# Attention and experts: all eight units in the attention loop, the first expert prepared inside it, POOL's small DMAs issued one by one

## The chip, the core and the metric

One core of a Trainium2 chip. TensorE (PE) multiplies, VectorE (DVE), ScalarE (ACT) and GpSimd (POOL) do the rest of the arithmetic, SyncE (SP) issues most of the DMAs, POOL the indirect ones. The metric is the device time of one execution in microseconds (us).

## What is computed

```python
def sm_attn(qq, kk, vv):
    s = scale * np.matmul(qq, kk.transpose(0, 1, 3, 2))
    s = s - np.max(s, axis=-1, keepdims=True)
    a = np.exp(s)
    a = a / (np.sum(a, axis=-1, keepdims=True) + 1e-09)
    return np.matmul(a, vv)
p_packed = sm_attn(p, k, v)              # 32 packed rows per head
x = sm_attn(q, p_packed, p_packed)       # 8 batches, 8 heads, 576 rows, 64 wide
# x as (4608, 512): row n is a token
logits = x @ w_gate + modality_bias[modality_id]
e_idx = np.argmax(logits, axis=1)        # 8 experts, one for each token
gate_w = softmax(logits)[arange(N), e_idx]
for e in range(E):
    h = np.maximum(x[e_idx == e] @ w1[e], 0.0)        # 512 to 1024
    out[e_idx == e] = gate_w[e_idx == e, None] * (h @ w2[e])
```

All is float32. With the inputs drawn here experts 4, 5 and 7 receive 2311, 1406 and 891 of the 4608 tokens, the other five none. By pairs of batches: 569 and 583 for experts 4 and 5 in the first pair; 589, 258 and 305 for 4, 5 and 7 in the second; 587 and 565 for 4 and 5 in the third; 566 and 586 for 4 and 7 in the fourth.

## The kernel before, in words

**Attention.** A batch is a *unit*; there are eight. Its steps are generators that emit a few instructions at each `next`: loads of k, q and v (`dk`, `dq`, `dv`, 1152 KB each), transposes of k and q on PE with copies by ACT (`k0..2`, `q0..2`), scores of the packed rows with max and exp (`c0`, `c1`), transposes of the weights (`a0..2`), the product with v (`p0`), its transpose (`t0`), the gate's product (`g0`), scores of q with a softmax of eight DVE steps and one ACT exp (`s0`, `s1`), the product that gives x, three tokens a step (`x0..2`, lines 318 to 333: PE, an ACT copy into the tile `xs`, a DVE copy of the logits into `lt`), and the store of x to the DRAM tensor `x_scr` (`w0`).

**The loop.** `ORDER` (line 353) is an order written out by hand for PE, DVE, ACT and SP: one round of it is one period, `>` is the unit after, `<` the unit before, and `e` is a place where one step of something else is emitted (the dictionary `more`). The loop runs it over six units (`NU = 2 * NA[1]`, line 692) and over the first steps of the two that follow. On the engines named in `manual_schedule` the instructions emitted inside keep their order; instructions emitted later are placed by the planner, also between these.

**Routing.** For each pair of batches `routing` (lines 368 to 428) computes the expert of each token and its place in the list of its expert: DVE steps, two or three small PE products for the ranks, DVE steps, an exp on ACT, and then nine indirect DMAs on POOL (line 420) that write 16 bytes for each of 128 tokens into the DRAM tensor `lst`. All nine are emitted at once.

**Slots.** The expert stage works in slots of 256 rows of one expert. `table_phase` (line 527) makes, with some fifty small DVE operations, a table of the slots that are full by then: table a from the first two pairs of batches (two slots), b from three pairs (four more), c from all (the rest; only here are slots that are not full, and one whose second half alone is filled is a half slot). `first_expert` (line 485) takes the expert with most tokens of the first pair; table a starts there, and the tables that follow start where the one before ended, in ascending order of experts, round. A slot is: `fetch` (line 614: POOL reads 256 rows of the list into `mt` and gathers the tokens into `xt` with four indirect DMAs), `st_x` (transposes into `x_hl` as a sum of two parts), `st_1` (96 products of 128x256; `st_1_half` 64 for a half slot), `st_2` (twice 24 products of 128x512, once for a half slot), and after each 24 an ACT step into `ot` (one buffer) and an indirect DMA of POOL into the output. `sw` loads and splits the weights of the next expert when it changes; `split_w` splits into two parts with ACT and DVE, for the very first W1 with ACT and POOL (line 612).

**The order around the change.** Behind the loop the kernel emits table a, the load of W2, the fetches of slots 0 and 1 and the split of W2, then what is left of units 6 and 7 (a second, shorter order, lines 826 to 831), their routing and the tables b and c, and the slots; the planner interleaves them. Till the end of the second attention part the slots have half the PSUM (`W["nh"] = 2`, one tile each of `ps_t` and `ps_o`). W1 of the first expert is loaded and split in the loop (`split_first`, line 719) as `e` steps.

## Time and profile before

| what | value |
|---|---|
| median of the runs | 676.68 us (676.12 to 677.13) |
| the profiled execution, its own time | 669.55 us |
| its span in the profile | 667.8 us |
| PE busy, share of the span | 590.3 us, 88% |
| PE's weight loads | 508.8 us, 76% |
| DVE, ACT, POOL busy | 254.4, 218.7, 203.0 us |

The span in 40 equal slices of 16.7 us, from the page (a digit is the busy share in tenths, 9 is 90% or more; PEclk is PE's granted clock in tenths of full speed):

```profile
PE   4979868767489978999999999999999999999990
POOL 3010050157652172222321334332233133223340
PEclk9989988967669998999999999999999999999996
DMA  9798896508932911111596212920111111113132
```

The first nine slices are the attention loop over six units. In slices nine to twelve PE's share and its clock are lower and POOL is busy; from slice sixteen on PE is busy throughout, and the transfers are few. Line numbers (L646 and so on) are those of the kernel printed above.

### The profile page before, as it was taken

How to read it: one execution, taken by the hardware profiler on the slowest of the kernel's cores; microseconds unless marked ns; L12 is line 12 of the kernel's file. 1: busy time of each engine (PE TensorE's matmuls, PEld its weight loads, DVE VectorE, ACT ScalarE, POOL GpSimd, SP SyncE). 2: the span in 40 equal slices, each digit the busy share in tenths (PEclk: the TensorE clock that was granted, in tenths of full speed). 3: DMA queues.
4: the chain of work that ended last, by engine and by line, in shares of the span. 5: the costliest groups of instructions: out<-in, count | busy, mean ns of one | idle time of the engine just before them, and what ended most of it. 6: DMA issues, size and time to landing. Idle time of an engine off the chain costs nothing. (4 is left out here: it accounts for less than half of the span.)

```text
span 667.8 us, 13143 instructions
## 1 busy us (share of the span) xinstructions
PE 590.3 (88%) x5108; PEld 508.8 (76%) x5108; DVE 254.4 (38%) x629; ACT 218.7 (33%) x369; POOL 203.0 (30%) x228
## 2 busy tenths in 40 slices
PE   4979868767489978999999999999999999999990
PEld 3657636526368968889888988899899889989980
DVE  2669948949635331112612017311121112012370
ACT  3747745636112202112612127221221222122450
POOL 3010050157652172222321334332233133223340
PEclk9989988967669998999999999999999999999996
DMA  9798896508932911111596212920111111113132
GB/s 297 241 378 322 300 312 194 184 11 251 255 96 75 294 48 60 49 48 33 132 278 207 64 57 87 257 65 34 49 50 48 49 49 42 41 48 49 47 54 34
DMA packets 38334, 86.66 MB, mean 130 GB/s; under 512 B 10400, under 2 KB 10400, under 8 KB 37216
## 3 DMA queue, kind: packets, MB, share of 16 engines
q1 hardware_dynamic: 27920, 63.39, 30.2%
q0 software_dynamic: 9264, 21.94, 11.8%
q8 instruction: 51, 0.84, 0.5%
q14 instruction: 43, 0.35, 0.2%
q10 hardware_dynamic: 1056, 0.15, 0.1%
HBM read 66.22 MB, written 19.24 MB: 128 GB/s over the span
## 5 line engine op out<-in xcount | busy, mean ns | idle before, releaser
L646 PE MATMUL ps_h<-x_hl,w1h 128*128 128x256 f32 x1088 | 203.7, 288 | 5.3 <-issue 4.4
L646 PEld LDWEIGHTS ps_h<-x_hl,w1h 128*128 128x128 f32 x1088 | 174.7, 195 | 11.2 <-issue 8.4
L646 PE MATMUL ps_h<-x_hl,w1l 128*128 128x256 f32 x544 | 156.1, 287 | 4.0 <-issue 4.0
L651 DVE SCALAR_TENSOR_TENSOR hl<-ps_h,hh 128x512 fp32r<-128x512 f32 x68 | 47.0, 691 | 263.9 <-ACT hh L650 258.8
L619 POOL DMA_INDIRECT xt<-x_scr,mt x92 | 91.0, 989 | 106.9 <-DMA mt<-lst 39.1
L680 PE MATMUL ps_o<-w2h,hh 128*128 128x512 f32 x296 | 118.0, 399 | 3.1 <-ACT ot L684 1.9
L680 PE MATMUL ps_o<-w2h,hl 128*128 128x512 f32 x296 | 116.5, 394 | 0.0
L680 PE MATMUL ps_o<-w2l,hh 128*128 128x512 f32 x296 | 115.8, 391 | 0.0
L646 PEld LDWEIGHTS ps_h<-x_hl,w1l 128*128 128x128 f32 x544 | 106.3, 195 | 2.7 <-issue 2.5
L650 ACT ACTIVATE hh<-ps_h 128x512 fp32r<-128x512 f32 x68 | 40.6, 597 | 172.1 <-PE ps_h L646 153.7
L685 POOL DMA_INDIRECT out_dram<-ot,mt x37 | 40.8, 1103 | 149.4 <-ACT ot L684 90.1
L684 ACT ACTIVATE ot<-ps_o,mt 128x512 f32<-128x512 f32 x37 | 25.4, 687 | 142.3 <-PE ps_o L680 110.6
L680 PEld LDWEIGHTS ps_o<-w2h,hh 128*128 128x128 f32 x296 | 55.7, 188 | 14.3 <-ACT ot L684 3.1
L680 PEld LDWEIGHTS ps_o<-w2h,hl 128*128 128x128 f32 x296 | 55.6, 188 | 11.4
L680 PEld LDWEIGHTS ps_o<-w2l,hh 128*128 128x128 f32 x296 | 55.7, 188 | 10.7 <-DVEq L809 0.2
L420 POOL DMA_INDIRECT lst<-meta,dsi x36 | 35.2, 977 | 68.2 <-DVE mxc L488 50.7
L208 ACT COPY kT<-ps 128x1024 f32<-128x1024 f32 (+1 forms) x48 | 36.8, 812 | 17.6 <-PE ps L204 17.4
L616 POOL DMA_DIRECT2D mt<-lst x23 | 17.3, 753 | 65.1 <-DMA out_dram<-ot,mt 52.6
L636 DVE TENSOR_TENSOR x_hl<-ps_t,x_hl 128x512 fp32r<-128x512 f32 x42 | 27.5, 683 | 22.9 <-ACTq L809 12.3
L325 PE MATMUL ps<-bd,a2T 64*64 64x136 f32 x576 | 25.1, 310 | 9.8 <-DVE gs L416 3.7
L633 PE MATMUL ps_t<-ident,xt 128*128 128x128 f32 x168 | 26.3, 280 | 6.1 <-DMA xt<-x_scr,mt 6.1
L325 PEld LDWEIGHTS ps<-bd,a2T 64*64 64x64 f32 x576 | 19.1, 147 | 14.2 <-issue 8.6
(188 smaller groups left out, 663.4 us busy)
## 6 DMA issues: line engine op xcount, KB each, us to landing
raw<-in_moe_w_dram SPq DMA_DIRECT2D x24, 512.0 KB
raw<-in_moe_w_dram SPq DMA_DIRECT2D x12, 1024.0 KB
rawk<-in_k_dram SPq DMA_DIRECT2D x8, 1152.0 KB
rawq<-in_q_dram SPq DMA_DIRECT2D x8, 1152.0 KB
rawv<-in_v_dram SPq DMA_DIRECT2D x8, 1152.0 KB
x_scr<-xs SPq DMA_DIRECT2D x8, 1152.0 KB
xt<-x_scr,mt POOLq DMA_INDIRECT x92
out_dram<-ot,mt POOLq DMA_INDIRECT x37
```

The source lines that it names most:

```text
L208: nc.scalar.copy(out=T_[:, w0:w0 + n].rearrange("p w n -> p (w n)"), in_=t[:, 0:n * P])
L325: nc.tensor.matmul(xp[64 * u:64 * u + 64, pr, z * XW:z * XW + XW], a2T[rs, u, 3 * m + z, :], bd[rs, u, :], start=True, stop=True)
L420: ins = ins_of(nc.gpsimd.indirect_dma_start(out=lst, out_offset=bass.IndirectOffsetOnAxis(ap=dsi[:, c:c + 1], axis=0), in_=meta[:, i * NC ...
L619: ins.append(nc.gpsimd.indirect_dma_start(out=xt[:, t, u * HW:u * HW + HW], out_offset=None, in_=x_scr[0:NA[ph] * 4 * S] if ph < 2 else x_scr,
L633: nc.tensor.transpose(out=ps[:, j], in_=xt[:, t, j * P:j * P + P], identity=ident)
L636: iv = tt(out=M["xl"][:, :, ts], in0=ps, in1=M["xh"][:, :, ts].bitcast(F32), op=ALU.subtract)
L646: nc.tensor.matmul(ps[:, f], M[a][:, j, (f0 + f) * P:(f0 + f) * P + P], M[b][:, j], start=(n == 0), stop=(n == 3 * KD - 1))
L650: ia = nc.scalar.activation(out=M["hh"][:, fs], in_=ps, func=AF.Relu)
L651: iv = nc.vector.scalar_tensor_tensor(out=M["hl"][:, fs], in0=ps, scalar=0.0, in1=M["hh"][:, fs].bitcast(F32), op0=ALU.max, op1=ALU.subtract)
L680: nc.tensor.matmul(op, M[a][:, j, t * P:t * P + P], M[b][:, j, :], start=(n == 0), stop=(n == 3 * KF - 1))
L684: nc.scalar.activation(out=ot, in_=op, func=AF.Copy, scale=mt.bitcast(F32)[:, t, 2:3])
L685: nc.gpsimd.indirect_dma_start(out=out, out_offset=bass.IndirectOffsetOnAxis(ap=mt[:, t, 1:2], axis=0), in_=ot, in_offset=None, bounds_che ...
```

## The change

All eight units go through the loop (`NU = 2 * NP`), with a new `ORDER`; the second attention part, with its own PSUM pools, is gone, and the slots have all their PSUM banks from the first on. `x`'s tile `xs` has one buffer instead of two. `first_expert` is gone: table a starts at expert 0 (`zero`). The steps of table a, the load of its first expert's W1, and the fetches of slots 0 and 1 are the `e` steps of period 5 (`table_first`), the four parts of the split of W1, the load of W2 and the transposes of slot 0 those of period 7 (`ready_first`). `routing` runs four times as `e` steps. Tables b and c are emitted behind the loop.

POOL's list writes and the five DMAs of a fetch are no longer emitted where they arise but put into `pending`; `feed` takes one from it (a fetch first if the lists that it needs are out) and ties it to the ACT instruction just emitted, so that POOL waits for that instruction. `feed` is called behind eight ACT steps of a period (`c0`, `c1`, `a0`, `s0`, `s1`, `x0` to `x2`) and behind the eight ACT steps of each of the first six slots. `flush` emits, without such a tie, what a slot still needs of its fetch, before the slot that precedes it.

```diff
+    pending = []
+    def feed(after=None):
+        if not pending:
+            return
+        lists = {z[0][1] for z in pending if z[0][0] == "list"}
+        n = next((n for n, z in enumerate(pending) if z[0][0] == "x" and not lists & set(range(need(z[0][1])))), 0)
+        for ins in pending.pop(n)[1]():
+            if after is not None:
+                tc.add_manual_dep(ins, getattr(after, "ins", after).name, SYNC, reason="one by one")
+    def flush(last=None):
+        while any(last is None or z[0][0] == "x" and z[0][1] <= last for z in pending):
+            feed()
+    def need(n):
+        return NA[0] if n < SA[0] else NA[1] if n < SA[1] else NP
...
-            nc.scalar.activation(out=st, in_=st, func=AF.Exp, scale=SCALE)
+            feed(nc.scalar.activation(out=st, in_=st, func=AF.Exp, scale=SCALE))
...
-    ORDER = (">>k1 <x2 <e >q2 s1 e s0 <e >q2 s0 >>k0 e >a2 s1 s1 >a0 s1 >a2 s0 s1 s0 >a1 s0 >q0 >a0 s0 s0 e >a1 <<w0 "
-             ">dv >p0 e <e >>k1 >c0 >>k0 >q1 >c1 >q0 x0 >q1 >p0 >p0 x1 >>c0 >t0 x0 >t0 x0 >>c0 x1 >>c1 >>>dk >>dq x1 "
-             ">t0 >s1 >g0 >>c0 >>>k2 >>c1 >>c1 >s1 >>c0 >s1 x2 >>c1 >g0 >s0 x2 e >s1 >s0 >>>k2 ")
+    ORDER = (">c0 <e t0 <x2 <e t0 >c0 <x2 >c1 >c0 >c0 s0 <e g0 >c1 <e >>>dk >c1 >c1 >>k2 g0 s0 <x0 <x0 >>k2 s1 <e s0 "
+             "s0 <x0 <x1 s1 >>k1 >q2 s1 <x1 s0 s1 <w0 <x1 >q0 e >q2 >a0 s1 s0 s1 e >a0 s1 >a1 >a1 >a2 s1 >>dq >>k0 s1 "
+             "s0 >a2 >>k1 >p0 s0 s0 >q0 >q1 >c0 >c1 >>k0 >p0 >p0 x2 >>dv >t0 >q1 e ")
...
         for c in range(NC):
-            ins = ins_of(nc.gpsimd.indirect_dma_start(
...
+            pending.append((("list", i), lambda c=c: scatter(i, c, dsi)))
...
-    def fetch(tb, s, ph, mt, xt):
+    def fetch(tb, s, ph, mt, xt, n):
         off = val(tb, s, 0, (ET.Pool,), 0, E * R - P2)
...
+        pending.append((("x", n), rows))
         for t in range(2):
             for u in range(2):
+                pending.append((("x", n), lambda t=t, u=u: part(t, u)))
...
-    NU = 2 * NA[1]
+    NU = 2 * NP
...
-        ZL["xs"] = actx.enter_context(tc.tile_pool(name="xsp", bufs=2))
+        ZL["xs"] = actx.enter_context(tc.tile_pool(name="xsp", bufs=1))
...
+        def table_first():
+            yield from table_phase("a", zero, NA[0], None, SA[0])
+            E0.append(val(T[0]["tab"], 0, 1, (ET.SP,), 0, E - 1))
+            load_w(W, 0, E0[0])
+            yield
+            for n in range(2):
+                pre(n)
+            yield
+        def ready_first():
             for z in range(4):
                 split_w(W, 0, nc.gpsimd, (z,))
                 yield
+            load_w(dict(raw2=W["raw1"]), 1, E0[0])
+            flush(0)
+            for t in range(2):
+                st_x(xts[0], W, (t,), ZL["ps1"])
+                yield
         E0 = []
-        more = {0: rest(), NU - 1: split_first()}
-        for n in range(NA[1]):
-            more[2 * n + 2] = route(n)
+        more = {0: rest(), 5: table_first(), 7: ready_first()}
+        for n in range(NP):
+            more[2 * n + 2] = routing(n, lts[n], ZL["ps1"])
...
-    W["t", 0] = pst.tile([P, KD, P], F32, name="ps_t0")
     for n in range(2):
-        W["h", n] = pst.tile([P, 2, P2], F32, name=f"ps_h{n}")
-    W["o", 0] = pst.tile([P, DM], F32, name="ps_o0")
-    W["no"] = W["nt"] = 1
-    W["nh"] = 2
-    with ExitStack() as actx:
...
-        u, prev = us[NU + 1], us[NU]
-        for z in "<x0 a0 a1 <x1 a2 <x2 <w0 p0 t0 g0 s0 s1".split():
-            run_all(prev if z[0] == "<" else u, z.lstrip("<"))
-        run_all(u, "x0 x1 x2 w0")
-        for _ in routing(NA[1], lts[NA[1]], ZL["ps1"]):
-            pass
-    T.append(table_phase("c", T[1]["last"], NP, T[1]["used"], None))
+        W["t", n] = pst.tile([P, KD, P], F32, name=f"ps_t{n}")
+        W["o", n] = pst.tile([P, DM], F32, name=f"ps_o{n}")
+    for n in range(4):
+        W["h", n] = pst.tile([P, 2, P2], F32, name=f"ps_h{n}")
+    W["no"] = W["nt"] = 2
+    W["nh"] = 4
...
     def slot(n):
...
+        slow[0] = n < SA[1]
...
         sw(n, 1)
         pre(n + 2)
+        flush(n + 1 if n < SA[1] else None)
```

## Rows read from the trace of the kernel before

**Rows 1.** Busy time by stage: length, busy us (instructions) per engine, PE clock, DMA share, GB/s

```profile
0.00:41.92 41.92, 28.32 (x382) 22.52 (x383) 19.40 (x50) 19.25 (x34) 8.86 (x36) 0.96 0.89 294
41.92:56.55 14.63, 13.78 (x272) 10.38 (x272) 11.87 (x25) 11.99 (x21) 0.00 (x0) 1.00 0.97 359
56.55:71.60 15.05, 14.13 (x280) 10.70 (x280) 13.49 (x33) 11.34 (x21) 0.00 (x0) 1.00 0.89 320
71.60:87.92 16.32, 14.20 (x275) 10.48 (x275) 15.27 (x42) 11.35 (x22) 0.00 (x0) 1.00 0.87 311
87.92:113.92 26.00, 19.42 (x280) 12.86 (x280) 15.21 (x45) 10.70 (x21) 8.87 (x9) 0.80 0.81 236
132.51:148.00 15.49, 9.55 (x138) 5.18 (x138) 5.98 (x41) 3.24 (x6) 8.97 (x9) 0.65 0.04 3
148.00:181.33 33.33, 19.99 (x214) 15.07 (x208) 26.48 (x87) 15.71 (x25) 20.95 (x16) 0.65 0.86 255
206.00:260.00 54.00, 48.47 (x347) 42.18 (x346) 17.15 (x78) 11.40 (x19) 20.09 (x21) 0.94 0.47 135
```

**Rows 2.** The chain of waits in order of time: start, us, what

```profile
412.60 11.76 PE ps_h L646 x96
622.15 7.69 PE ps_h L664 x64
```

**Rows 3.** PE's groups by line: two rows of 0 to 412.4, one of 412.4 to 668

```profile
L646 PE MATMUL ps_h<-x_hl,w1h 128*128 128x256 f32 x512 | 99.7, 293 | 4.5 <-issue 4.4
L664 PE MATMUL ps_h<-x_hl,w1h 128*128 128x256 f32 x32 | 7.7, 283 | 0.0
...
L646 PE MATMUL ps_h<-x_hl,w1h 128*128 128x256 f32 x576 | 104.1, 283 | 0.8 <-ACTq L863 0.8
```

**Rows 4.** Timeline of PE at the last expert switch: start, us, what, [idle before, releaser]

```profile
637.80 0.35 PE L664 MATMUL ps_h<-x_hl,w1h 128*128 128x256 f32 x1 [1.64 <-DVE w1l L612]
```

**Rows 5.** Timeline of POOL, PE and DVE around the second burst of lists

```profile
133.49 0.98 POOL L420 DMA_INDIRECT lst<-meta,dsi  x1 [3.83 <-DVE ex_s L482]
...
143.94 0.96 POOL L420 DMA_INDIRECT lst<-meta,dsi  x1 [0.30 <-issue]
...
142.57 1.29 PE L217 MATMUL ps<-kT,ppT 64*32 64x320 f32 x16 [3.71 <-issue]
...
146.42 0.76 DVE L226 TENSOR_REDUCE mx<-ps 128x1 f32<-128x576 f32 x1 [4.79 <-remote]
```

**Rows 6.** DMA queues from 133 to 147 us: packets, MB, share of 16 engines

```profile
q0 software_dynamic: 288, 0.02, 2.2%
q8 instruction: 1, 0.02, 1.3%
```

**Rows 7.** Timeline of POOL and DVE at the split of W1

```profile
150.13 7.50 POOL L612 TENSOR_TENSOR w1l<-raw,w1h 128x1024 fp32r<-128x1024 f32 x3 [5.23 <-ACT w1h L611]
...
155.70 2.55 DVE L312 TENSOR_TENSOR st<-st,dn 128x576 f32<-128x576 f32 x1
...
161.02 0.76 DVE L312 TENSOR_TENSOR st<-st,dn 128x576 f32<-128x576 f32 x1
```

**Rows 8.** Timeline of DVE: first and last step of a table, 48 rows between

```profile
232.60 0.16 DVE L529 TENSOR_TENSOR cnt<-run,base 128x8 f32<-128x8 f32 x1
...
241.57 0.15 DVE L507 CAST tab_c<-tab_f 128x7 int32<-128x7 f32 x1
```

**Rows 9.** Timeline of POOL: gathers for one slot of the steady state

```profile
604.22 0.75 POOL L616 DMA_DIRECT2D mt<-lst  x1 [2.45 <-DMA out_dram<-ot,mt]
607.08 0.99 POOL L619 DMA_INDIRECT xt<-x_scr,mt  x1 [2.11 <-DMA mt<-lst]
...
610.89 0.95 POOL L619 DMA_INDIRECT xt<-x_scr,mt  x1 [0.30 <-issue]
```

**Rows 10.** Timeline of DVE: first step of a routing, and the one behind its ranks

```profile
226.81 0.23 DVE L376 TENSOR_TENSOR lg<-ps,bias_all 128x72 f32<-128x72 f32 x1
...
232.18 0.23 DVE L403 TENSOR_TENSOR dst<-ps,run 128x72 f32<-128x72 f32 x1 [1.82 <-PE ps L400]
```

More of the change, by code (lines that the diff above doesn't have):

```diff
@@ L363, in ins_of @@
         return getattr(x, "ins", x)
-    scattered = [[] for _ in range(NP)]
     def routing(i, lt, ps1):
@@ L687, in st_2, with slot_of, pre @@
             bounds_check=N - 1, oob_is_err=False)
+        if slow[0]:
+            feed(ia)
     lts = [sm.tile([P, 2, 2, NC, E], F32, name="lt", bufs=2) for _ in range(NP)]
-    NU = 2 * NA[1]
+    NU = 2 * NP
+    mxp = ctx.enter_context(tc.tile_pool(name="mx", bufs=1))
+    mts = [mxp.tile([P, 2, 4], I32, name=f"mt{n}") for n in range(4)]
+    xts = [mxp.tile([P, 2, DM], F32, name=f"xt{n}") for n in range(2)]
+    W["x"] = mxp.tile([P, KD, 2, P2], F32R, name="x_hl")
+    W["xh"], W["xl"] = W["x"][:, :, 0], W["x"][:, :, 1]
+    first = (0, SA[0], SA[1])
+    T = []
+    slow = [False]
+    def slot_of(n):
+        ph = sum(n >= z for z in first[1:])
+        return T[ph]["tab"], n - first[ph], ph
+    def pre(n):
+        if n < NS_:
+            fetch(*slot_of(n), mts[n % 4], xts[n % 2], n)
     with ExitStack() as actx:
@@ L768, in packed_attn_moe_kernel @@
         W["2" + z] = wpool.tile([P, KF, DM], F32R, name="w2" + z)
-    first = (0, SA[0], SA[1])
-    def slot_of(n):
-        ph = sum(n >= z for z in first[1:])
-        return T[ph]["tab"], n - first[ph], ph
-    def pre(n):
-        if n < NS_:
-            fetch(*slot_of(n), mts[n % 4], xts[n % 2])
-    for n in range(2):
-        pre(n)
     def sw(n, which, after=()):
@@ L789, in go @@
         def go():
[L790 to L794 removed]
+            if n or which:
                 split_w(W, which)
```

153 lines of the change are left out of this document (66 added, 87 removed).

## The prediction, made before the change was built

> **What bounds the kernel now.** I read the table of busy times by stage first, with windows cut at the starts of the x products of successive units [rows 1]. It shows three stages. Up to 87.92 us TensorE (PE) is the bound of the attention loop: a unit takes 14.63 us, 15.05 us and 16.32 us, PE is busy for 13.8 to 14.2 us of each, the clock is 1.00, the DMA share is 0.87 to 0.97. From 87.92 to 260 the kernel loses time: in 132.51 to 148.00 PE is busy for 9.55 of 15.49 us at a clock of 0.65, in 148.00 to 181.33 for 19.99 of 33.33 us at 0.65, and even where expert slots already run (206 to 260) 5.5 of 54 us are idle. From 412.60 on PE is the bound again, in the plainest way: the chain of waits is PE alone, slot after slot [rows 2].
>
> From that the value of everything ahead can be read. Between 412.60 and 622.15 [rows 2] 576 of the first kind of product are made, 64 for each full slot of 256 rows, so nine slots [rows 3]: 209.55 / 9 = 23.28 us a slot. A half slot is 637.80 - 622.15 - 1.64 (a wait for the split of W1) = 14.01 us [rows 2, 4]. Before 412.4 there were 512 / 64 = 8 full slots and 32 / 32 = one half slot [rows 3]. So the expert stage is worth as much as if it had run alone and without a gap from 412.60 - 8 x 23.28 - 14.01 = 212.3, less up to 1.64 us for the split after its half slot: **211 us**. The eight units of attention need, at 13.8 us of PE each, some 110 us of PE. The 211 us are therefore about 90 us of attention that does not fill PE, and that is what the change is about.
>
> **What the change does to that mark.** After it the expert stage begins when the eighth unit is through the loop. The number of slots stays: routing of these inputs gives experts 4, 5 and 7 2311, 1406 and 891 rows, in both orders 17 full and 3 half slots. Starting at expert 0 instead of the fullest one makes the order 4, 5, 7 with two switches where there were 5, 7, 4, 5 with three; the two after a half slot (1.64 us, [rows 4]) stay, the one that goes followed a full slot, which covers it. So I count nothing there (bounds: a gain of 1.6, nothing lost). The time after is today's time minus (211 - the new start of the expert stage). The start, term by term:
>
> The x product of unit 0 starts at 41.92 [rows 1]. At the pace without lists (14.63, then three pairs of 15.05 + 16.32, since each pair of units carries one routing) that of unit 7 starts at 41.92 + 14.63 + 94.11 = **150.7 us**. The order string is new, so the same pace is an assumption; PE's work of 13.8 us a unit bounds it below, at 41.92 + 7 x 13.8 = 138.5. A period carries the first steps of the next two units as well, and behind units 6 and 7 there are none; against that the DVE steps of unit 7 itself must still be walked through. I take **-4** (0 to -12).
>
> The first expert's table moves into the loop. Its DVE steps took, for another table, from 232.60 to 241.57 [rows 8], 9 us among other work. In a period with routing DVE is busy for 15.27 of 16.32 us [rows 1], so it has 1 us left there and some 3 us in the others: **+3** (0 to 9). The instructions of the fullest expert's choice go away in return.
>
> W1's split on POOL: three of its operations took 7.50 us, and a DVE operation that takes 0.76 us took 2.55 us beside them [rows 7]. Four of them now fall into the last period, where DVE's chain is what unit 7 waits for: **+4** (0, if PE's work covers it, to 4 x 1.8 = 7.2).
>
> The lists. Nine list writes follow each other today, one every 1.31 us, from 133.49 to 144.90 [rows 5]; between 138.9 and 146.4 PE and DVE run dry: PE waits 3.71 us for "issue", DVE 4.79 us for "remote", which is no work of another engine of this core [rows 5]. It is not bandwidth: the DMA share in that stretch is 0.04 [rows 1], and what moved was 288 packets of the lists and, on the queue of instructions shown there, one block of 0.02 MB [rows 6]. I read it as instruction blocks that come late while the lists are being written. With the first burst the period was 26.00 us instead of 16.32 (with the load of W1 in it), so 9.7 us a burst is the upper price. Afterwards each list waits for one of the eight ACT steps of a period, one per some 1.8 us (14.63 / 8) instead of 1.31, and the fetches get their turn in the gaps. Nothing is queued behind the waiting list on POOL but other lists, gathers, and the four splits. For the 27 lists of the loop: **+4** (0 to 29).
> The Trainium skill ("Runtime: NRT & Kernel Launch", section "Instruction fetch mechanics") says that each engine streams its instructions in blocks of 16 KiB through a DMA queue of its own and that the crossing is mostly hidden. By that rule lists would cost nothing and the sum would be 4 us lower. The trace does not agree: these waits of 3.71 and 4.79 us stand in a stretch without other traffic.
>
> From unit 7's x product to the first expert product: two x products, and the last routing, whose DVE steps and PE products took 5.4 us from 226.81 to 232.18 [rows 10] and stand ahead of the slot in PE's order if the planner leaves them there: **+6** (1 to 8). The rows of slot 0 are gathered a period earlier and cost nothing; were they late, it would be the chain of the steady state, 604.22 to 611.84 = 7.6 us [rows 9].
>
> Clock: the last period has little PE work, as 148.00 to 181.33 has today, at 0.65 [rows 1]; a few us of slot 0 will run at the lower of the two levels: **+2** (0 to 11.5, a whole first half of a slot lost again).
>
> The first slots have to carry the split of W2, two tables and the lists of the last pair: today 5.5 us are lost in 206 to 260 [rows 1]; with four banks for the first product from the start PE can run ahead: **+2** (0 to 9).
>
> x's staging tile has one buffer instead of two. The store of unit n must have landed before unit n + 1 copies into it, more than half a period later by the order string; its 1152 KB at the 359 GB/s of [rows 1] are 3.3 us. I cost it at nothing; if it waits behind one load of the same size, 3.3 us a unit come on top, which belongs to the upper end.
>
> Sum: 150.7 - 4 + 3 + 4 + 4 + 6 + 2 + 2 = **167.7 us**. Gain: 211 - 167.7 = **43.3 us**. The profiled execution took 669.55 us (its span is 667.8), so 626.3 by its own measure; the median of the runs is 676.68, 7.1 us above it, so **633.4 us**.
>
> **Rivals.** *The lists starve the engines singly as they do in a burst.* For it: no list stands without its neighbours in this trace. Against it: PE's wait begins 5.4 us after the burst's first list, at 138.86. At 9.7 us for each of three bursts' worth (29 instead of 4): 633.4 + 25 = 658 us. Chance 0.14.
> *The loop is better than today's.* The pace nears PE's own work (138.5 instead of 150.7 - 4), the lists cost nothing and DVE keeps up: 8 + 4 + 5 = 17 us less, 616 us or below. Chance 0.14.
> *Slower: the gathers of the first six slots lose their cover.* They go through POOL one item per ACT step, behind the output write of the slot before. If in each of the six slots the whole chain of 7.6 us plus the landing of the last gather (2.1 us, by the wait for the list rows, [rows 9]) is waited for, that is 58 us, and 691 us. It decides from 43.3 / 6 = 7.2 us uncovered per slot. Against it: the change issues what is left of a slot's gathers at once before the slot that precedes it, and 11.76 us of products [rows 2] lie between. Chance 0.06.
> *The change doesn't do what it says*: POOL's order is the planner's, and the manual waits could leave bursts as they are. That is the first rival's price, and in it.
>
> **How the numbers follow.** Forecast 633.4 with 0.64 (616 to 650), starving lists 0.14 (650 to 665), better loop 0.14 (603 to 616), uncovered gathers 0.06 (650 to 700), all else near no change 0.02. The range that leaves out about 0.2 is 610 to 656. Faster by over 0.2% (about what a measurement of this kernel can tell from no change): 0.93; within 0.2%: 0.02; slower: 0.05.
>
> **What would show it.** First expert product near 168 us instead of 181.33 (and then without attention between); eight x products with periods near 15 us and no period of 26 us; waits for "issue" and "remote" in the loop under 0.5 us each; lists on POOL with an ACT step ahead of each; from the first slot on 23.3 us a slot; the end of PE 441 us after the first expert product (17 x 23.28 + 3 x 14.01 + 2 x 1.64). Wrong would be the forecast if periods stay near 14.6 us and PE still idles at the change from loop to slots, or if slots 0 to 5 take over 25 us.

## The result, and the profile after

| | before | after |
|---|---|---|
| median of four runs each, one chip | 676.40 us (674.98 to 677.13) | 658.57 us (658.08 to 659.48) |
| ratio | | 0.974 (95%: 0.972 to 0.976) |
| profiled execution, its own time / span | 669.55 / 667.8 us | 658.44 / 656.7 us |
| PE busy | 590.3 us | 577.6 us |

The kernel became 17.8 us faster. The forecast was 43.3 us faster (633.4, range 610 to 656). The sign was right, the size less than half, and the time lies 2.6 us above the range. The profiled execution of before lay 7 us below the median of its runs and that of after does not, so the two traces differ by only 11.1 us.

PE now ends at 640.8; 441 us of gapless slots (17 x 23.28 + 3 x 14.01 + 2 x 1.64, the prediction's own figure) counted back from there begin at 199.8. The forecast was 167.7. So **32.1 us are missing**, and the trace says where. First the loop, windows of after from the x product of unit 0 to that of unit 7 (length, then busy us and instructions of each engine, clock, DMA share, GB/s), answering [rows 1]:

```profile
core 0: us, PE busy (x) PEld busy (x) DVE busy (x) ACT busy (x) POOL busy (x), PEclk, DMA share, GB/s
39.88:55.06 15.18, 14.23 (x276) 10.61 (x276) 13.19 (x27) 11.33 (x21) 3.20 (x6) 1.00 0.69 230
55.06:69.85 14.79, 14.21 (x279) 10.69 (x279) 13.71 (x36) 11.31 (x20) 0.00 (x0) 1.00 0.92 329
69.85:86.45 16.60, 14.35 (x275) 10.54 (x275) 15.84 (x46) 11.41 (x21) 4.27 (x4) 1.00 0.83 297
86.45:102.97 16.52, 15.04 (x280) 10.98 (x279) 13.24 (x32) 11.21 (x20) 5.04 (x5) 1.00 0.77 268
102.97:121.50 18.53, 14.28 (x276) 10.59 (x275) 17.50 (x57) 12.50 (x22) 4.02 (x4) 1.00 0.74 247
121.50:144.75 23.25, 16.54 (x261) 12.04 (x262) 19.79 (x76) 8.38 (x16) 5.20 (x5) 0.78 0.66 160
144.75:167.70 22.95, 4.78 (x127) 3.15 (x126) 21.14 (x83) 8.94 (x13) 14.95 (x11) 0.69 0.23 79
```

Read the length against the busy time of PE, then of DVE. The first four periods end at 102.97, where the forecast's bare pace (41.92 + 14.63 + 15.05 + 16.32 + 15.05) has 102.97 as well. That it fits to a hundredth is chance: the first x product starts 2.04 us earlier and the four periods take 2.04 us longer. Nine lists are written in the third and fourth of them (78.55 to 97.32, some of them right behind each other), and no instruction of DVE or PE waits as much as 1 us for "remote" or "issue". The last three take 64.73 us instead of 47.69, that is 2.2, 8.2 and 6.6 us more than 16.32, 15.05 and 16.32; in them DVE is busy for 17.50 of 18.53, 19.79 of 23.25 and 21.14 of 22.95 us, while PE falls to 4.78 of 22.95 and the clock to 0.69. PE's two longest waits in them end on DVE. Single instructions, timeline of after (start, duration, engine, line, what, and in brackets the idle time before it and its releaser):

```profile
129.29 1.29 PE L237 MATMUL ps<-kT,ppT 64*32 64x320 f32 x16 [5.15 <-DVE tab_f L564]
...
167.70 1.64 PE L347 MATMUL ps<-bd,a2T 64*64 64x136 f32 x24 [16.95 <-DVE a2T L337]
...
178.16 0.77 PE L678 MATMUL ps_h<-x_hl,w1h 128*128 128x256 f32 x2
...
155.74 0.80 ACT L352 COPY xs<-ps 128x768 f32<-128x768 f32 x1 [5.65 <-remote]
...
158.15 7.47 POOL L629 TENSOR_TENSOR w1l<-raw,w1h 128x1024 fp32r<-128x1024 f32 x3 [0.56 <-ACT w1h L628]
...
148.08 0.16 DVE L548 SCALAR_TENSOR_TENSOR rem<-used_a,cnt 128x8 f32<-128x8 f32 x1
...
156.97 0.14 DVE L574 CAST pre_b<-pref 1x1 int32<-1x1 f32 x1
...
160.85 2.55 DVE L334 TENSOR_TENSOR st<-st,dn 128x576 f32<-128x576 f32 x1
...
164.14 1.50 DVE L331 TENSOR_SCALAR dn<-dn 128x18 f32<-128x18 f32 x1
...
195.38 1.23 DVE L629 TENSOR_TENSOR w2l<-raw,w2h 128x1024 fp32r<-128x1024 f32 x1 [14.47 <-issue]
...
172.92 3.06 SPq L614 DMA_DIRECT2D raw<-in_moe_w_dram  x4
183.59 0.35 SPq L358 DMA_DIRECT2D x_scr<-xs  x1
...
227.17 0.76 POOL L641 DMA_DIRECT2D mt<-lst  x1 [4.22 <-DMA lst<-meta,dsi]
```

In order of time: PE waits 5.15 us for table a, whose steps DVE runs in one row from 122.72 to 128.37. Table **b**, which the forecast had in the first slots, was put by the planner between 148.08 and 156.97, among the first steps of unit 7's softmax on DVE. ACT stands 5.65 us for "remote" before a copy into `xs`. DVE's steps of unit 7 take 2.55 and 1.50 us beside the split of W1 on POOL (answering [rows 7]). So unit 7's x product starts at 167.70, 17.0 us behind the bare pace and **10.0 us** behind the forecast's 157.7. The first expert product follows 10.46 us later instead of 6: **4.5 us**. From there to the gapless start are 21.6 us instead of 4: **17.6 us**, the largest part. Windows of after over this last stretch, the same columns:

```profile
178.16:190.00 11.84, 11.84 (x79) 11.84 (x78) 2.37 (x16) 4.65 (x7) 1.94 (x2) 0.74 1.05 242
190.00:200.00 10.00, 4.17 (x32) 3.55 (x30) 4.62 (x11) 1.89 (x4) 4.30 (x4) 0.89 0.21 63
200.00:210.00 10.00, 8.35 (x30) 6.80 (x31) 7.05 (x38) 0.69 (x1) 0.00 (x0) 0.77 0.76 241
...
230.00:240.00 10.00, 8.14 (x39) 5.58 (x38) 1.38 (x2) 1.87 (x3) 7.80 (x8) 1.00 0.31 92
240.00:250.00 10.00, 7.47 (x52) 6.64 (x51) 0.66 (x1) 1.28 (x2) 5.30 (x6) 0.95 0.23 66
250.00:260.00 10.00, 10.00 (x66) 9.55 (x65) 3.30 (x6) 2.76 (x5) 4.09 (x5) 0.88 0.14 38
```

PE idles 5.83 us in 190 to 200, where W2's split (`w2l`) comes after a 14.47 us wait, 1.65 in the next ten, 1.86 in 230 to 240 for the rows of the third slot, whose list read on POOL waits until 227.17, and 2.53 in 240 to 250: 11.9 us. The last of these is no wait for rows. Inside the third slot's first product PE waits several times for "issue" between single products, while ACT stands for "remote" and POOL issues lists, a gather and an output write (241.60 to 246.43):

```profile
245.00 0.28 PE L678 MATMUL ps_h<-x_hl,w1h 128*128 128x256 f32 x1 [0.70 <-issue]
...
248.71 0.60 ACT L682 ACTIVATE hh<-ps_h 128x512 fp32r<-128x512 f32 x1 [6.18 <-remote]
```

The clock takes most of the rest: (1 - clock) x PE's busy time gives 3.1, 0.5, 1.9, 0.4 and 1.2 us in the rows below 1.00, 7.1 us in all (an estimate). From 260 on PE is full and a slot takes about 23.3 us, as forecast.

### The profile page after: what moved, and what is told of

Read it like the earlier page. It is cut to its first block, busy times and chain, and to the rows that moved or that the text cites. A ratio compares the mean times of both kernels' runs of the same rounds, so it can differ in the third digit from the quotient of the medians.

```text
span 656.7 us, 13061 instructions
## 1 busy us (share of the span) xinstructions
PE 577.6 (88%) x5108; PEld 504.3 (77%) x5108; DVE 246.8 (38%) x615; ACT 211.7 (32%) x361; POOL 202.6 (31%) x229
## 5 line engine op out<-in xcount | busy, mean ns | idle before, releaser
L678 PE MATMUL ps_h<-x_hl,w1h 128*128 128x256 f32 x1088 | 201.4, 287 | 3.8 <-issue 2.2
L719 POOL DMA_INDIRECT out_dram<-ot,mt x37 | 39.2, 1060 | 164.7 <-ACT ot L718 83.2
L718 ACT ACTIVATE ot<-ps_o,mt 128x512 f32<-128x512 f32 x37 | 25.5, 688 | 184.5 <-PE ps_o L714 147.3
L224 PE MATMUL ps<-ident,rawk 128*128 128x128 f32 x144 | 23.1, 308 | 8.3 <-DMA rawk<-in_k_dram 6.7
L666 DVE TENSOR_TENSOR x_hl<-ps_t,x_hl 128x512 fp32r<-128x512 f32 x40 | 25.7, 683 | 11.0 <-ACT ot L718 8.6
## 6 DMA issues: line engine op xcount, KB each, us to landing
rawk<-in_k_dram SPq DMA_DIRECT2D x8, 1152.0 KB, 10.8
rawv<-in_v_dram SPq DMA_DIRECT2D x8, 1152.0 KB, 11.1
```

Source lines behind the costliest of these rows:

```text
L224: nc.tensor.transpose(out=t[:, w * P:w * P + P], in_=raw[:, (w0 + w) * P:(w0 + w) * P + P], identity=ident)
L666: iv = tt(out=M["xl"][:, :, ts], in0=ps, in1=M["xh"][:, :, ts].bitcast(F32), op=ALU.subtract)
L678: nc.tensor.matmul(ps[:, f], M[a][:, j, (f0 + f) * P:(f0 + f) * P + P], M[b][:, j], start=(n == 0), stop=(n == 3 * KD - 1))
L718: ia = nc.scalar.activation(out=ot, in_=op, func=AF.Copy, scale=mt.bitcast(F32)[:, t, 2:3])
L719: nc.gpsimd.indirect_dma_start(out=out, out_offset=bass.IndirectOffsetOnAxis(ap=mt[:, t, 1:2], axis=0), in_=ot, in_offset=None, bounds_che ...
```

## The experiments

The kernel before took 673 to 676 us in the first comparison and on three chips below, and 645 us on two others. So each ratio is to before on its own chip, and times of different chips aren't subtracted.

| run | chip | us | ratio (95%) |
|---|---|---|---|
| e1_table_b_late | second, before 674.86 | 660.34 | 0.981 (0.977 to 0.985) |
| e2_lists_held | second | 657.77 | 0.976 (0.971 to 0.980) |
| e3_w1_held | second | 655.85 | 0.972 (0.967 to 0.976) |
| e4_gathers_held | second | 663.70 | 0.985 (0.980 to 0.989) |
| e5_split_dve | third, before 644.95 | 650.09 | 1.007 (1.003 to 1.011) |
| e6_two_lists | third | 648.44 | 1.004 (1.002 to 1.007) |
| e7_routing_late | third | 649.20 | 1.005 (1.001 to 1.008) |
| e8_all | third | 645.78 | 1.000 (0.997 to 1.003) |
| b_again (before) | fourth, before 675.90 | 676.74 | 1.001 (0.998 to 1.004) |
| a_again (after) | fourth | 658.16 | 0.976 (0.972 to 0.980) |
| e9_lists_early | fourth | 641.02 | **0.948** (0.945 to 0.951) |
| e10_xs_apart | fourth | 641.62 | 0.952 (0.948 to 0.955) |
| b_third (before) | fifth, before 673.08 | 672.85 | 1.000 (0.997 to 1.002) |
| a_third (after) | fifth | 660.05 | 0.982 (0.979 to 0.986) |
| e8_again (as e8_all) | fifth | 649.94 | 0.968 (0.963 to 0.972) |
| e11_table_b_moved | fifth | 643.59 | 0.957 (0.954 to 0.961) |
| e12_no_ties | sixth, before 644.91 | 653.28 | 1.014 (1.011 to 1.018) |
| b_fourth (before) | sixth | 645.15 | 1.000 (0.998 to 1.003) |

The theories at the start: DVE's work in the last periods delays unit 7 (rival: instruction waits beside POOL's lists do); W2's split waits for the store of `x`, which stands behind the next expert's W1 loads on SP (rival: again the lists).

**Table b out of the loop** (after the last routing, in the manual order):

```diff
-    for _ in table_phase("b", T[0]["last"], NA[1], T[0]["used"], SA[1] - SA[0]):
-        pass
...
             for m in sorted(more):
                 for _ in more[m]:
                     pass
+            for _ in table_phase("b", T[0]["last"], NA[1], T[0]["used"], SA[1] - SA[0]):
+                pass
```

> The second table's some fifty VectorE steps, which the changed kernel runs between 148.1 and 157.4 us beside the softmax of the last unit, are written behind the last routing instead. Theory A (VectorE has too many steps in the last attention period): the first x product of the last unit comes 4 to 7 us earlier than 167.70, the first expert product at 171 to 174 in place of 178.16, and the time is 652 to 655 us. Theory B (ScalarE waits for its instructions, 5.65 us until 155.74, while the gathers run, and VectorE only filled that time with table steps): the x product stays within 2 us of 167.70 and the time at 657 to 660 us.

Unit 7's x product came at 165.47, 2.2 us earlier than in after (1.1 earlier than in its repeat a_again), and the last period still took 24.2 us: ACT's copies into `xs` waited 2.66 us for the store of the unit before and 3.02 us for "remote". The time, 660.34, did not fall. The table's some 50 steps alone were not the cause. The wait of `w2l` got its name here:

```profile
193.45 1.23 DVE L629 TENSOR_TENSOR w2l<-raw,w2h 128x1024 fp32r<-128x1024 f32 x1 [17.59 <-DMA x_scr<-xs]
```

**The lists of slot 0's first product held back** behind its last ACT step:

```diff
+            hh_last[0] = ia
...
-        slow[0] = n < SA[1]
+        slow[0] = 0 < n < SA[1]
         if n < SA[1]:
             st_1(W)
+            slow[0] = True
+            for _ in range(4 if n == 0 else 0):
+                feed(hh_last[0])
```

> In the first slot the four list writes that stand behind one ScalarE step each (184.55 to 194 us) all wait for the fourth and last of these steps instead, so that none runs between 176 and 193 us. Theory B (list writes hold back VectorE's instructions): VectorE's wait of 14.47 us ahead of its first W2 split step shrinks below 5 us and TensorE's idle time at 192 to 204 us (about 6 us) goes; the time is 651 to 655 us. Theory C (that step waits for the last unit's x store, whose memory the split W2 is written to, and which is queued behind the next expert's W1 load on SyncE): the wait stays at 13 to 16 us, the time at 657 to 662 us.

Without lists in that stretch `w2l` still came at 193.16, released by the same store, issued at 181.87. The lists are not what it waits for. (Its wait was only 7.0 us here, since unit 7's x product came at 174.29, 6.6 us later than in after: DVE steps of 0.1 to 0.2 us lasted 2.2 to 2.6 us beside the split of W1 on POOL.)

**The next W1 load held back** behind slot 0's first product (`sw(0, 0)` emitted there, its DMAs tied to the last ACT step):

```diff
+                    for h in held:
+                        tc.add_manual_dep(ins_of(ins), h.name, SYNC, reason="behind the first product")
...
-    sw(0, 0)
...
-            st_1(W)
+            ia, _ = st_1(W)
+            if n == 0:
+                held.append(ia)
+                sw(0, 0)
+                held.clear()
```

> The load of the next expert's W1, 2.1 MB, waits for the fourth hidden step of the first slot; on SyncE's queue the last unit's x store then stands ahead of it. Theory C (the first W2 split step waits for the x store): the store is issued near 175 us in place of 183.59, the step starts at 184 to 188 in place of 195.38, TensorE's idle time at 192 to 204 goes, and the time is 651 to 655 us. Theory B (list writes hold back VectorE's instructions): the step still starts at 193 to 197 and the time is 657 to 661 us.

Timeline of this kernel, SP, DVE, POOL, PE:

```profile
174.60 0.35 SPq L358 DMA_DIRECT2D x_scr<-xs  x1
...
184.18 1.23 DVE L631 TENSOR_TENSOR w2l<-raw,w2h 128x1024 fp32r<-128x1024 f32 x1 [3.70 <-ACT hh L684]
...
220.25 0.76 POOL L643 DMA_DIRECT2D mt<-lst  x1 [9.40 <-DMA lst<-meta,dsi]
...
229.96 0.69 PE L665 MATMUL ps_t<-ident,xt 128*128 128x128 f32 x2 [8.21 <-DMA xt<-x_scr,mt]
```

The store leaves at 174.60 instead of 183.59, `w2l` comes 11 us earlier and PE is full from 190 to 220. That shows the cause: the split waits for the last store of `x`, and that store stood on SP behind the W1 loads (in after SP waits 7.4 us for the landing of a weight load before it). That W2's low part lies in the memory that `xs` had is taken from the order of the buffers here; e10 below shows it. But of this a few us at most arrive in the time (ratio 0.972, after has 0.974 to 0.982 on other chips): now the third slot's rows are late, PE is busy for 1.79 us of 220 to 230. The list read waits 9.40 us for the landing of the last list; the lists were written one per ACT step, the last two of them behind the output writes of the first slot.

**The gathers of the first two slots held back** behind the last exponential (and with them the lists that stand in `pending`):

```diff
-        if not pending:
+        if not pending or hold[0]:
             return
+        after = after or gate_[0]
...
+            hold[0] = True
             for n in range(2):
                 pre(n)
...
+            if b == NU - 1 and u == 1:
+                hold[0], gate_[0] = False, ins
             feed(ins)
```

> The row fetch and gathers of the first two slots wait for the last softmax exponential of the last unit and come behind the W1 split on GpSimd (from about 168 us in place of 146.79 to 174.9). Theory B (gathers hold back ScalarE's instructions): the wait of 5.65 us ahead of the copy at 155.74 goes, and the first x product of the last unit comes 3 to 6 us earlier than 167.70. Theory A (VectorE's own steps and the W1 split beside them set it): it stays within 1.5 us of 167.70. The first slot's rows come late by it in both, first expert product 182 to 188 us, and the time is 662 to 668 us.

ACT's "remote" wait of 5.65 us went, and a long step came on DVE. Timeline, DVE and POOL:

```profile
159.77 6.47 DVE L337 TENSOR_SCALAR dn<-dn 128x18 f32<-128x18 f32 x1
...
159.26 6.94 POOL L635 TENSOR_TENSOR w1l<-raw,w1h 128x1024 fp32r<-128x1024 f32 x3
```

A step of 128x18 lasted 6.47 us, as long as three of POOL's splits. Unit 7's x product came at 170.25, 2.6 us later than in after, where neither theory had it, and the first expert product only at 194.32, behind the late gathers. With the next run this names the second cost of the last period.

**The rest of W1's split on DVE**, behind unit 7's softmax:

```diff
-            for z in range(4):
-                split_w(W, 0, nc.gpsimd, (z,))
-                yield
+            yield
+            yield
+            split_w(W, 0, nc.vector)
+            yield
```

> The rest step of the W1 split, four pieces, runs on VectorE behind the last unit's softmax instead of on GpSimd beside it. Theory A2 (GpSimd's split pieces hold VectorE's steps up: 2.55 and 1.06 us where 0.76 and 0.18 do, and in the kernel with the gathers held one step of 0.13 took 6.47 us): no step of that softmax takes over 0.85 us, and the first x product of the last unit comes at 161 to 165 us in place of 167.70; with some 5 us of split pieces on VectorE behind it and the last routing ahead of the first expert product, that product is at 174 to 177 (178.16) and the time 654 to 658 us, since the wait for the x store and the late rows of the third slot stay. Rival (ScalarE's wait for instructions beside the gathers sets the x product): it stays at 166.5 to 169.

Timeline of DVE, the same steps as above:

```profile
157.81 0.18 DVE L331 TENSOR_SCALAR dn<-dn 128x18 f32<-128x18 f32 x1
158.02 0.27 DVE L332 RECIPROCAL dn<-dn 128x18 f32<-128x18 f32 x1
158.32 0.76 DVE L334 TENSOR_TENSOR st<-st,dn 128x576 f32<-128x576 f32 x1
```

0.18 and 0.76 us instead of 1.06 and 2.55. The x product came at 162.00 and the first expert product at 171.31 (in after, on another chip, 167.70 and 178.16), while `w2l` still waited (191.09, 17.04 us for the store). What the split on POOL costs can be read on one chip: the last period takes 24.9 and 25.9 us with it (e6, e7 below) and 21.4 and 21.0 without (e5, e8) on the third chip, 25.5 (a_again) and 21.5 and 20.0 (e9, e10) on the fourth, 25.2 (a_third) and 20.0 (e8_again) on the fifth. That is about 4 to 5 us (an estimate, since these runs differ in other edits too, most of which act behind this period). Against before the kernel is now 0.7% *slower*, because before took 645 us on this chip: the first sign of the question that the last runs are about.

**Two lists per step in slot 0** (with e3's edit):

```diff
-            if slow[0]:
+            for _ in range(slow[0]):
                 feed(ia)
...
-        slow[0] = n < SA[1]
+        slow[0] = 2 if n == 0 else int(n < SA[1])
```

> On top of the kernel with the held W1 load (655.85 us): in the first slot two pieces of GpSimd's work are put behind each ScalarE step instead of one, so that the third pair's nine lists stand ahead of the slot's first output scatter on GpSimd. Theory D (the third slot's rows come late because its last two lists stand behind the two output scatters of the first slot, at 201.64 and 209.88 us, and so their fetch at 220.25): that fetch comes at 198 to 206 us, TensorE's idle time at 219 to 246 us (10.6 us) falls below 4, and the time is 646 to 650 us. Rival B (the list writes cost as much wherever they stand, by holding back instructions): idle time of 4 to 8 us appears at 184 to 200 instead, and the time is 654 to 658.

The third slot's list read came at 203.30 (220.25 in e3), but still behind a 10.14 us wait for the last list's landing. PE still waits there, from 211.8 on, 3.85, 2.42 and 2.40 us for the rows of one gather after the other: the gap came earlier and did not go.

**The last routing and table c inside slot 0** (with e3's edit; two steps of the routing behind each group of products):

```diff
-        for n in range(NP):
+        for n in range(NP - 1):
             more[2 * n + 2] = routing(
...
+            st_1(W, routing(NP - 1, lts[NP - 1], banks()) if n == 0 else iter(()))
```

> On top of the kernel with the held W1 load (655.85 us): the last pair's routing and the third table are worked out inside the first slot, between the pieces of its products, instead of ahead of them. Theory E (the routing chain of VectorE and TensorE stands between the last x product, over at 173.7, and the first expert product at 177.74): the first expert product comes at 173.5 to 175. As the late rows of the third slot are not touched, that gain of 3 to 4 us is waited away at 219 to 246 us if they hang on the lists' own chain: 653 to 657 us in all; if they move along, 651 to 653.

The first expert product came 5.0 us behind unit 7's x product; in e6, on the same chip, it was 9.5. So the last routing ahead of the slot costs 4.5 us. What it brings to the time can't be read, as e3 was not run on this chip; PE is busy for 2.31 us of 220 to 230 in it.

**All four edits** (e3, e5, e6, e7):

> The four edits together: next W1 load held, W1's rest step on VectorE behind the softmax, the last routing inside the first slot, two pieces behind each step of the first slot. If each removes its own wait, the first x product of the last unit comes at 161 to 165 us, the first expert product at 169 to 173, no idle time over 3 us stands at 184 to 250 us, and the time is 636 to 643 us. If GpSimd's small transfers cost instructions wherever they stand, idle time of 8 us or more is left in the first four slots and the time is 646 to 652 us.

x product 160.10, first expert product 165.92, near the forecast's 157.7 and its sum without the last 4 us, 163.7. Yet PE is busy for 4.28 us of 200 to 210, waiting 7.86 us for the rows of the third slot. Repeated on the fifth chip, to have e8 on a chip where before is slow:

> The kernel with the four edits, which took 645.78 us on the chip where the kernel before took 644.95. Theory F: on a chip where that takes about 675, it has 5 to 15 us of waits named remote or issue on ScalarE and VectorE that it did not have there, and takes 647 to 656 us; on a quick chip it repeats 644 to 647. Rival G: the ratio of 1.000 to the kernel before repeats.

There PE is busy for 10.97 us of 200 to 220. The time, 649.94, is 10.1 us below that of after on the same chip (a_third, 660.05), and it lies where theory F had it; but the 5 to 15 us of waits for "remote" or "issue" that were to bring it there are not in the trace. ACT and DVE have none up to 300 us, although eight lists follow each other at 180.93 to 190.92. What remains is the lists' turn in POOL's order; e9 tests that.

**The repeats of both kernels** on the fourth chip:

> The kernel before, unchanged, with a profile on the same chip as the other kernels of this group. On the chip of the first experiments it took 674.86 us, on that of the second ones 644.95. Theory F (chips differ in how long an engine waits for its instructions while GpSimd's small transfers run): where it takes about 645 us, its waits named remote or issue at 118 to 160 us sum to under 5 us and the x products of its units 5 to 7 come 20 to 30 us earlier; where it takes about 675 the profile repeats the one shown, with some 18 us of such waits. Rival G (chips differ in the clock that they grant to TensorE): the granted clock of the run differs from 0.95 and the difference lies in the expert slots after 300 us.

> The changed kernel, unchanged, beside the kernel before on the same chip. Theory F: where the kernel before takes about 675 us, 656 to 660 (0.974); where it takes about 645, the waits that the spaced lists avoid are not there to be avoided, and what the change added (the split beside the last softmax, the x store behind the W1 load, the late rows of the third slot) is left: 650 to 655 us, 1.008 to 1.016, slower than before. Rival G: the same ratio 0.974 on either chip, 628 us where before takes 645.

They agree with the first comparison: 676.74 and 658.16 us. So does after on the fifth chip (a_third): 660.05 us, where before takes 673.08.

**The lists of the third pair early** (e3, e5, e7; and everything still pending issued right behind the gathers, not one per step):

```diff
-            flush(0)
+            while pending:
+                feed()
...
-        flush(n + 1 if n < SA[1] else None)
+        flush(2 if n == 0 else n + 1 if n < SA[1] else None)
```

> As the kernel with the four edits, but the third pair's nine lists follow the gathers on GpSimd at once in the last attention period, with no ScalarE step ahead of each, and the third slot's row fetch follows them. Theory D: the lists run at about 157 to 172 us, the third slot's rows are there before 200 us, TensorE's idle time of 7.9 us ahead of the third slot goes, and the time is 5 to 9 us under the 645.8 of that kernel where the kernel before takes 645 (637 to 641). Theory B (lists one behind another hold back instructions): waits of 4 to 8 us named remote or issue appear on ScalarE or VectorE at 157 to 175 us and the first expert product is at 170 to 175 instead of 165.9.

```profile
170.00:180.00 10.00, 7.29 (x66) 5.92 (x59) 1.36 (x5) 3.59 (x4) 7.56 (x9) 0.83 0.95 314
180.00:190.00 10.00, 7.86 (x46) 7.32 (x46) 5.80 (x11) 3.44 (x6) 3.55 (x5) 0.66 0.29 79
190.00:200.00 10.00, 10.00 (x60) 8.61 (x60) 6.47 (x29) 2.38 (x4) 3.55 (x4) 1.00 1.00 311
200.00:210.00 10.00, 10.00 (x69) 9.11 (x68) 3.88 (x34) 1.28 (x3) 4.12 (x5) 1.00 0.72 156
```

In these windows PE is full from 190 on and stays so. The third pair's last list is written at 181.04, the third slot's list read comes at 185.72, and no wait for rows is left. 641.02 us, 17 us below after on the same chip and 35 below before. This is the best ratio of the study. Theory D's sign came, and theory B's in part: the first expert product is at 171.09, and there are waits for "remote", DVE 7.7 us ahead of `lg` (until 184.16, behind the lists that now follow each other again) and ACT 8.0 us ahead of `ot` (until 232.56, where PE is full).

**`xs` apart from `w2l`** (e9, with the next W1's buffer set up last, so that it and not `w2l` takes the memory of `xs`):

> As the kernel before it in this list, with the buffer of the next W1 set up last, so that it and not the split W2 lies on the memory of the last x store. Theory C: the first W2 split step waits for the W2 load alone and starts 2 to 4 us earlier, TensorE's wait of about 4 us for it in the first slot goes, and the time is 2 to 4 us lower. Rival: W2's own load sets that step (its second half lands at 174.7, the store's end is seen at 177.4), and the time is within 1.5 us.

```profile
174.01 1.28 DVE L631 TENSOR_TENSOR w2l<-raw,w2h 128x1024 fp32r<-128x1024 f32 x1 [6.28 <-issue]
...
179.74 0.34 SPq L358 DMA_DIRECT2D x_scr<-xs  x1
...
180.64 0.74 PE L392 MATMUL ps_t<-lt,fold 128*64 128x72 f32 x4 [8.94 <-issue]
```

`w2l` starts 10.6 us earlier than in e9 (184.63) and before the store of `x` is even issued: that shows that the shared memory had tied the two. But there is no gain in time: 641.62. Now the load of W2 itself is what the split waits for (DVE waits 7.7 us for "issue" before `w2l`), the split stands on DVE ahead of the last copies of the logits (`lt`), and PE, which needs these for the routing, waits 8.94 us and is busy for 1.70 us of 170 to 180. The rival held for the time.

**Table b behind the softmax and W1's split** (on top of e10):

> As the kernel with the buffers set apart (641.62 us beside 675.9 before), with the second table's steps behind the last unit's softmax and the W1 split on VectorE. Theory H (VectorE's steps set the last attention periods; it was busy 17.95 of the last one's 20.04 us, some 7 of them the table's): the last period, from the first x product of the seventh unit to that of the eighth, shrinks by 4 to 6 us to 14 to 16 and the time by 2 to 5. Rival (the chain copy of xs, exponential, softmax sets it, with waits of ScalarE for its instructions): it shrinks by under 2 us, and the time is within 2.

The last period took 20.1 us, in e10 20.04. With the split gone from POOL the number of DVE's steps is not what sets this period; ACT's copies into `xs` wait 2.82 us for the store and 5.01 us for "remote". That theory fell a second time.

**No ties** (after, with `feed` not tying an instruction to an ACT step):

```diff
-        for ins in pending.pop(n)[1]():
-            if after is not None:
-                tc.add_manual_dep(ins, getattr(after, "ins", after).name, SYNC, reason="one by one")
+        pending.pop(n)[1]()
```

> The changed kernel without the ties of GpSimd's lists and gathers to ScalarE's steps: they run as soon as their data is there, one right behind another. Theory I (spacing them is what keeps the instruction waits of VectorE and ScalarE at 12 us in the first 300 us, where the kernel before has 40 to 57): these waits rise to 25 to 60 us and the time to 662 to 674. Rival J (the ties cost as much as they save, since they bring the third pair's lists behind the first slot's output scatters): the third slot's rows are fetched before 200 us, TensorE's idle time at 219 to 250 goes, and the time is 648 to 657.

On this chip there are no "remote" waits without ties either, so theory I's sign did not come. The x product of unit 7 comes at 172.73, behind 22.30 us of idle PE, and one DVE step says why:

```profile
160.08 11.69 DVE L332 TENSOR_TENSOR st<-st,dn 128x576 f32<-128x576 f32 x1
```

It takes 0.76 us elsewhere; here it stands beside all four splits of W1 on POOL (160.32 to 171.15). The third slot's rows are gathered from 175.27 to 180.11, no wait for them is left, and PE is full from 210 on, as rival J had it. After was not run on this chip, so what the ties are worth, on either kind of chip, stays open.

**Before on the fifth and sixth chip**, to see what differs between 673 and 645 us:

> The kernel before, unchanged, with a profile. Theory F (chips differ in how long an engine waits for its instructions while GpSimd's small transfers run): about 675 us with 40 to 60 us of waits named remote or issue on VectorE and ScalarE in the first 300 us, or about 645 us with under 10 us of them. Rival G (the granted clock): about 645 with the same waits and a clock over 0.96.

> The kernel before, unchanged, with a profile. Theory F: about 675 us with 40 to 60 us of waits named remote or issue on VectorE and ScalarE in the first 300 us, or about 645 with under 10 us of them. Rival G: about 645 with the same waits and a granted clock over 0.96.

The waits of before up to 300 us (engine and instruction <- releaser: us in total, times, longest), first on the slow chip:

```profile
ACT hh L650 <- remote: 16.2, 1, 16.2
DVE mx L226 <- remote: 15.5, 3, 6.0
...
ACT xs L330 <- remote: 12.5, 2, 9.0
...
ACT ot L684 <- issue: 10.6, 3, 3.8
...
ACT ppT L279 <- remote: 8.5, 2, 5.0
...
ACT x_hl L635 <- issue: 7.8, 1, 7.8
```

and all that ACT and DVE have there on the quick one:

```profile
ACT ot L684 <- issue: 14.4, 4, 3.8
...
ACT xs L330 <- issue: 3.4, 1, 3.4
```

With the smaller ones these are 75 us against 18. The waits for "issue" are alike (19 and 18); the difference is "remote", 56 us against none (41 and 48 in the two other traces of before, on chips where it takes 676 us), and on the slow chip all of those over 2 us begin within a burst of nine lists. The period with the first burst of lists takes 26.0 us on the slow chip (x products at 90.45 and 116.46) and 16.1 on the quick one (91.20 and 107.29) (forecast without lists: 16.32). Part of that is given back: the period after it takes 18.6 and 23.0 us, so that 5.6 us are left over both. The next one, with the second burst, takes 30.1 and 21.5. So what the prediction read as late instructions beside the lists ([rows 5]) is there on one kind of chip and not on the other, with the same program, and its 9.7 us a burst is too high. Rival G fails: from 300 us on the granted clock is 1.00 in both traces, and 20.4 of the 26.9 us between the two spans arise ahead of the last x product (224.16 and 203.78). In the trace of after these waits of ACT and DVE add up to 11.9 us for "remote" and 3.6 for "issue" besides that of `w2l`.

## Why the prediction went wrong

**What held.** The worth of what lies ahead is read from the gapless start; 23.3 us a slot from 260 on, the order 4, 5, 7 and two switches came as said. The bare pace held up to unit 4 within 2 us (to a hundredth by luck), and beside the lists there no wait of DVE or PE reached 1 us. One figure on the way is wrong by its own numbers: 211 - 8 x 13.8 leaves 101 us of attention that does not fill PE, not "about 90"; nothing was worked out from it.

**Term by term**, 32.1 us:
- The start of unit 7 (-4 + 3 + 4 + 4 = 7): 17.0 us, 10.0 more. By period it is 2.2, 8.2 and 6.6. The 8.2 are the period with table a, taken at 3 (within its bound of 9): DVE runs the table's steps in one row, and PE waits 5.15 us behind them. That it is the table is read from this trace alone; no run took it out. The saving of 4 did not come. The split on POOL was taken at 4 and is worth about that; it can block DVE for as long as it runs (6.47 us in e4, 11.69 in e12). Table b was counted in the first slots, and the planner put it in the last period; but e1 and e11 show that taking it out is worth 2.2 us or nothing. The store of `x` through one buffer was costed at nothing: ACT waits for it, 0.53 us in the trace of after and 2.9 and 3.1 in its repeats (the given upper price was 3.3 a unit). The term of the lists, 4, is near the 5.65 us of "remote" by luck and not by its mechanism: that wait stands beside the gathers of the first slots, and it is gone in e4 and e8_again.
- From the x product to the first slot (+6, 1 to 8): 10.46. The last routing was counted (5.4 us) and is worth 4.5 (e6 against e7). Too small was what stands beside it, 0.6 us: without the routing 5.0 us are left in e7, for the x products and the transposes of slot 0.
- The first slots (+2, and +2 for the clock): 21.6. **This is the step that failed by most.** 11.9 us of it are idle PE, some 7.1 the lower clock behind its gaps (taken at 2, within its bound of 11.5), 2.6 are not accounted for. The prediction counted the load of the next W1 nowhere, and it priced a store of `x` behind a load only for the reuse of `xs`: the load stands on SP ahead of the last store, that store holds W2's split (7.5 us of idle PE), and e3 removes this wait. Behind it stands a second one that the prediction named as the rival of uncovered gathers but for all six slots: the third slot's rows alone come late (1.86 us in after, 8.21 us in e3), since their list read waits for the last list. Each of the two hides the other: e3 gains little, and e8, in which W2's split still holds PE up for 4.0 us and the rows for 9.1 (e8_again), is 10.1 us below after on one chip. In e9 neither is left, and it is 17.1 us below. Both of them also move the split of W1 and the routing, so these gains are not those of the two waits alone: of the 14.5 us between the two profiled executions of e9 and a_again, 5.3 are the earlier first expert product (171.09 against 176.41), and 9.1 are won behind it. The third piece, 2.53 us at 244 to 249, stays open.

**The rivals.** The starving lists (650 to 665) gave the right time, 658.57, for another reason: in the loop no wait of PE or DVE for "remote" or "issue" over 1 us stands beside them, and what looks like it at 244 to 249 is worth 2.5 us. The uncovered gathers held for one slot of six and didn't turn the sign.

**The rule on instruction blocks** (the Trainium skill, "Runtime: NRT & Kernel Launch", section "Instruction fetch mechanics": blocks come through a DMA queue and the crossing is mostly hidden): the trace of the quick chip does not speak against it, with no wait for "remote"; on the others 41 to 56 us of such waits stand, which would speak against it if they are late blocks. That late instruction blocks are the cause of "remote" and "issue" was argued in the prediction and is still not shown; shown is that in before the waits for "remote" stand at POOL's bursts of lists and differ by chip. A burst alone does not bring them even on a slow chip, as e8_again shows.

**What this says of the change.** The gain of 1.8 to 2.6% is shown in three comparisons, all where before takes 673 to 676 us. On the quick chips after itself was not run; two kernels close to it, e5 and e12, were 0.7% and 1.4% slower than before. That the change gains only where those waits are is thus likely and left open, and so is what e9 does on a quick chip.

## What to carry to other kernels

Follow every DMA that shares a queue with a moved one, those that are emitted unchanged too: here a load that nobody had touched stood ahead of a store, and that store held a buffer that lay on the same memory. When two late things end at nearly the same point, removing either shows next to nothing; look at what PE waits for after each removal before calling a cause small. And compare on one chip only: the same program took 645 and 676 us.

## What the runs showed of the hardware

- The chips differ by 4 to 5% for one program, and in three traces of before by 41 to 56 us of waits of ACT and DVE for "remote" against none in the one of a quick chip; the mean clock is 0.935 on a slow chip and 0.961 on a quick one, and 1.00 on both from 300 us on.
- A DVE step of 128x18 that takes 0.18 us took 6.47 us beside three POOL operations of 128x1024 in a row, which took 6.94 us; one of 128x576 that takes 0.76 us took 11.69 us beside four (e12). The Trainium skill ("GPSIMD Engine Reference", section "Specifications") says that GpSimd's interface to SBUF is shared with VectorE, with contention for some forms of VectorE's instructions. The traces agree in that, and give the price that the page does not.
- A POOL read of `lst` waits for the landing of the last list write, whose own time on POOL is 0.96 us: 3.7 and 4.2 us in e9 and after, where the DMA share of that stretch is 0.29 and 0.53, and 4.8, 9.4, 10.1 and 10.8 us in e7, e3, e6 and e8_again, where it is 0.97 to 1.06.
